# Attention and a squared-ReLU MLP in one kernel: transposes by row halves in the second half, other visits in the MLP

## The chip, the cores and the metric

The kernel runs on one core of a Trainium2 chip. The metric is the device time in microseconds (us) of one launch. TensorE is called PE here (its weight loads PEld), VectorE DVE, ScalarE ACT, GpSimd POOL, and SP is the engine that issues most DMAs. Each engine takes its instructions in the order of its own queue.

## The reference, cut to what matters

Four batches, eight heads, 576 positions, head size 64. A bias that depends on the distance of two positions goes through a tiny network (1 to 32 to 8) and is added to the scores; softmax; product with v. The result, 2304 tokens by 512, goes through a two-layer MLP with ReLU and a square between.

```python
scores = scale * np.matmul(q, k.transpose(0, 1, 3, 2)) + bias
attn = np.exp(scores - np.max(scores, axis=-1, keepdims=True))
x = np.matmul(attn / (attn.sum(-1, keepdims=True) + 1e-9), v)   # -> (2304, 512)
h = x @ w_in                                                   # (512, 2048)
out = np.maximum(h, 0) ** 2 @ w_out                            # (2048, 512)
```

## The kernel before, in words

**Attention.** An item is one batch, one pair of heads and one block of query rows. A full item has 128 rows of each of the two heads (two score tiles of 128x576); the last 64 rows of both heads make one tail item (one tile). Items are numbered by `s`. The first half (batches 0 and 1, items 0 to 39) also builds the bias. The second half (batches 2 and 3, items 40 to 79) takes its order from an explicit list: for each of eight groups (head pair, batch) four full items F and a tail T. Transposes and value products there go in pairs of items: at an even step `s`, after the scores of item `s`, PE transposes the exponentials of items `s-2` and `s-1`, ACT copies the results to SBUF (`pt`), and at step `s+1`, after the scores of item `s+1`, PE multiplies both with v (`px`). In ten items the pairs are FF, FF, TF, FF, FT, here named (0,1), (2,3), (T,0), (1,2), (3,T).

Four PSUM banks, tags a to d, serve the second half. Before, the four head groups of 128x128 transposes of a pair go to banks a, b, c and again a, the two blocks that straddle the heads (`pa`, L521) go to bank d, and `px` is written to bank d afterwards; DVE takes `px` out (L578). The scores hold four further banks, and only one item has room in them: the scores of the next item wait until DVE has read the last (L438). DVE writes its result to one of two buffers `t`, which ACT's exponential (L445) frees. In the first half, one item at a time, the transposes are already done by row halves (`transposes_by_rows`, `half_block`, L534): a 128x128 block is transposed as two blocks of 64 rows, from rows 0 to 63 into one bank and from rows 64 to 127 into another.

**Jobs.** Between these steps the second half runs a list of jobs, filled into each step by a budget of ACT and DVE time (`fill`): scanning w_in for its largest value, the normalisation of each group, the splitting of early w_in tiles (`in_job`: `lead`, `sums_in`, `high_in`, `low_in`) and of two w_out tiles (`out_job`) into a high and a low part, and the splitting of x of batches 0 and 1 (`x_scaled`: sums on POOL, high parts on ACT, low parts on DVE). A destination of such a part lies in the bias area and is free only when the items that read that bias are done (`dest_at`).

**MLP.** An item of the MLP, a visit, is one batch `n` of 256+256 tokens (or the tails of all) and one `P`: two w_in tiles of 128x512 and two w_out tiles. `products` does 42 matmuls of 256 columns (a seven-product scheme for 2x2 blocks, each operand in a high and a low part), `sums` (ACT and DVE) combines them, `squares` (ACT) does ReLU and square, `parts_g` splits the result (`gh` on ACT, `gl` on DVE), and `down` does 24 matmuls of 512 columns into `y`. In iteration `i` PE does `products(i)` and then `down(i-1)`. Beside them `lead_at` says which weight tile is prepared in an iteration, `largest_at` where the largest of an x is found, `split_at` where an x is split. A batch is visited twice where not all weights are there yet: `runs` lists batch, first P, end P. The w_in tiles that are not early are fetched one at a time into one buffer (`zw`), each after `low_in` of the one before.

Of the kernel before, what the change touches and what calls it, by code (L numbers as in the profile page):

```python
# [10 lines left out]
F32 = mybir.dt.float32  # L11
# [37 lines left out]
NE = 8  # L49
# [28 lines left out]
def attention_then_relu2_mlp(ctx: ExitStack, tc: tile.TileContext, q, k, v, cols, w_in, w_out, psi, xmat, dist, out):  # L78
# [422 lines left out]
    def transposes(us, tags=None):  # L501
        next_tag = iter(tags) if tags else None
        groups = []
        pa = None
        for m, u in enumerate(us):
            p_of = p_t.pop(u)
            pt = att.tile([128, 9, 128], F32, name="pt", tag="pt", bufs=2)
            pt_t[u] = pt
            for h in range(2 if units[u][2] < TAIL else 1):
                groups.append((p_of, pt, h))  # L510
            groups.append((p_of, pt, None, m))
        if len(us) > 1:
            heads = [g for g in groups if g[2] is not None]
            groups = heads[:3] + [g for g in groups if g[2] is None] + heads[3:]
        last = []
        for p, pt, h, *m in groups:
            if h is None:
                if pa is None:
                    pa = bank("pa", "d" if tags and len(us) > 1 else next(next_tag) if tags else None)
                at = slice(128 * m[0], 128 * m[0] + 128)  # L520
                PE.transpose(pa[:, at], p[:, S - 64:S + 64], ident)  # L521
                last.append((pt[:, 8], pa[:, at]))
                if len(last) == len(us):
                    yield from last
            else:
                pp = bank("pp", next(next_tag) if tags else None)
                for c in range(4):
                    k0 = h * (S + 64) + 128 * c
                    PE.transpose(pp[:, 128 * c:128 * c + 128], p[:, k0:k0 + 128], ident)  # L529
                yield pt[:, 4 * h:4 * h + 4], pp.rearrange("p (c m) -> p c m", c=4)  # L530

# [4 lines left out]
    def transposes_by_rows(u):  # L536
# [11 lines left out]
        yield pt[:, 8], pa  # L548

# [433 lines left out]
    def norm_job(u):  # L983
# [6 lines left out]
            ("ROW", 0.24, lambda: st.update(rows=norm_copy(norm_rows(st["parts"], "cb"[row_step[1] - 1]))), u + TL + 1, lambda: now[0] % 2 == 0 and row_left()),  # L990
# [32 lines left out]
    def scaled(ps_col):  # L1023
        wscale.extend(power_of(ps_col))
        for n in range(AB):
            job(now[0] + 1, ("DVE", 0.16, lambda n=n: power_job(now[0] + 1, overall(xcols[n]), lambda c: x_scaled(n, c)), lambda n=n: sum(x[0] == n for x in x_found) == HP))

    xcols = [column(HP) for _ in range(AB)]
# [3 lines left out]
    def x_job(at, n):  # L1032
        job(at, *(("DVE", 0.67, lambda c=c: x_found.append((n, x_largest(n, xcols[n], (c,))))) for c in range(HP)))

    def x_scaled(n, ps_col):
        scale_of(n, ps_col)
        if n == 0:
            place_x = raw_tile("w2")
            free = [place_x[:, 512 * k:512 * k + 512] for k in range(2)]
            for k, ms in enumerate(((3, 1, 7), (4, 6), (2, 5))):  # L1040
                stages = []
                for m in ms:
                    if RIGHT[m][1]:
                        sum_at[m] = free[k].rearrange("p (c t) -> p c t", c=2)
                        stages.append(("POOL", 1.3, lambda m=m: sums_x(0, (m,))))
                    stages.append(("ACT", 0.71, lambda m=m: high_x(0, (m,))))
                    stages.append(("DVE", 0.74, lambda m=m: low_x(0, (m,))))
                jobs.insert(len(norms), [max(now[0], first[groups[AB * HP + AB]] + 1), stages])
        else:
            free = [a.rearrange("p (c t) -> p c t", c=2) for a in (take(1, 4480, 512), take(0, 9856, 512))]  # L1050
            for k, ms in enumerate(((3, 1, 7), (4, 6), (2, 5))):
                stages = []
                for m in ms:
                    if RIGHT[m][1]:
                        sum_at[n, m] = free[k]
                        stages.append(("POOL", 1.3, lambda m=m: sums_x(n, (m,))))
                    stages.append(("ACT", 0.71, lambda m=m: high_x(n, (m,))))
                    stages.append(("DVE", 0.74, lambda m=m: low_x(n, (m,))))
# [53 lines left out]
    with tc.manual_schedule():  # L1112
# [5 lines left out]
        for s in range(NA, NU + TL + 3):  # L1118
# [17 lines left out]
            if s % 2 == 0:  # L1136
# [3 lines left out]
                for m, c in enumerate(transposes(us, iter("bacb" if s == NA else "abca")) if us else ()):  # L1140
                    ACT.copy(*c)  # L1141
# [283 lines left out]
```

## Time and profile before

| | us |
|---|---|
| median of 3 runs | 696.8 (696.4 to 697.21) |
| the profiled execution | 697.57 |
| its span in the trace | 695.8 |
| PE busy | 676.8 (97%) |
| DVE busy | 549.9 (79%) |
| ACT busy | 473.2 (68%) |
| POOL busy | 196.5 (28%) |

The span runs from the first instruction to the last; the execution's time holds 1.8 us more around it. Busy is the time in which an engine had at least one instruction under way. Matmuls overlap each other, so that PE is called busy also where the next matmul starts late; rates are therefore read from the starts of instructions.

### The profile page before, as it was taken

To read this page: it belongs to the slowest core of one execution; us is meant where nothing else is said; L and a number is where in the kernel's file an instruction comes from. 1 tells how busy PE (TensorE), PEld (TensorE's weight loads), DVE (VectorE), ACT (ScalarE), POOL (GpSimd) and SP (SyncE) were. 2 spreads that over 40 slices of the span, in tenths; PEclk is the share of its full clock that TensorE was granted. 3 is DMA by queue.
4 is the path that set the end of the run, shared out by engine and by line. 5 is a ranking of instruction groups with operands and counts; after the bars stand their busy time and mean duration, and the time that the engine had idled before them with its cause. 6 is when DMAs were issued, how large, how long until landed. Compare 5 with 4: busy or idle time off the path is not lost.

```text
span 695.8 us, 17950 instructions
## 1 busy us (share of the span) xinstructions
PE 676.8 (97%) x7238; PEld 561.5 (81%) x7238; DVE 549.9 (79%) x1165; ACT 473.2 (68%) x960; POOL 196.5 (28%) x313
## 2 busy tenths in 40 slices
PE   6899999999999999999999999999999999999997
PEld 5578888887877878778788888888888888888886
DVE  8999989877788898998888969777477775567664
ACT  5678888888777989997666756766466664447221
POOL 6465545442112343653223205112020112001000
PEclk9999999999999999999999999999999999999999
DMA  6740000017476134111901443050057222633101
GB/s 188 205 128 13 20 2 3 2 63 206 152 266 196 55 116 131 47 33 57 367 2 62 152 167 122 14 214 1 1 194 291 106 77 106 227 121 122 62 1 31
DMA packets 31682, 75.16 MB, mean 108 GB/s; under 512 B 5616, under 2 KB 13936, under 8 KB 30576
## 3 DMA queue, kind: packets, MB, share of 16 engines
q1 hardware_dynamic: 31440, 73.76, 31.1%
q8 instruction: 57, 0.93, 0.6%
q14 instruction: 25, 0.20, 0.1%
q10 hardware_dynamic: 160, 0.26, 0.1%
HBM read 55.66 MB, written 18.35 MB: 106 GB/s over the span
## 4 chain that ended last, share of the span: by engine, by line
PE 86%; DVE 8%; ACT 2%; issue 2%; POOL 1%; DMA 0%; ACTq 0%; POOLq 0%; DVEq 0%
PE y L1302 29%; PE ha L1210 13%; PE sp L425 11%; PE px L565 10%; PE hb L1210 10%; PE bb L383 5%; PE pp L529 3%; PE pp L534 3%; DVE t L438 2%; DVE mask L373 1%; PE pa L547 1%; ACT pt L1141 1%; DVE bt L391 1%; ACT p L445 1%; DVE xT L496 0%
## 5 line engine op out<-in xcount | busy, mean ns | idle before, releaser
L1210 PEld LDWEIGHTS <-area 128*128 128x128 f16 x1680 | 147.7, 98 | 25.3 <-issue 8.4
L1302 PE MATMUL y<-w,gh 128*128 128x512 f32 x576 | 149.0, 398 | 0.6 <-ACT gh L1246 0.6
L1302 PEld LDWEIGHTS y<-w,gh 128*128 128x128 f32 x576 | 105.1, 188 | 22.2 <-ACT gh L1246 1.3
L438 DVE CUSTOM_DVE_ANT_0 t<-sp,area 128x576 f32<-128x576 f32 x144 | 104.2, 753 | 21.2 <-PE sp L425 10.3
L445 ACT ACTIVATE p<-t,negm 128x576 f32<-128x576 f32 x144 | 112.9, 794 | 2.7 <-DVE negm L438 2.1
L425 PE MATMUL sp<-k,q 64*128 64x288 f32 (+1 forms) x640 | 99.4, 428 | 5.5 <-DVE negm L438 3.9
L565 PE MATMUL px<-pt,v 128*64 128x128 f32 (+1 forms) x1600 | 92.2, 266 | 0.0
L565 PEld LDWEIGHTS px<-pt,v 128*64 128x64 f32 x1600 | 79.2, 137 | 10.7 <-ACT pt L1141 6.0
L1210 PE MATMUL ha<-area 128*128 128x256 f16 (+1 forms) x816 | 85.1, 260 | 0.7 <-DVE c L1227 0.7
L399 POOL TENSOR_TENSOR area<-bt,bt 128x256 f32<-128x256 f32 x72 | 65.9, 922 | 64.1 <-DVE bt L391 63.9
L1302 PE MATMUL y<-w,gl 128*128 128x512 f32 x288 | 79.0, 390 | 0.0
L425 PEld LDWEIGHTS sp<-k,q 64*128 64x128 f32 (+1 forms) x640 | 53.3, 176 | 25.5 <-issue 6.0
L1210 PE MATMUL hb<-area 128*128 128x256 f16 (+1 forms) x612 | 64.7, 260 | 0.0
L1302 PEld LDWEIGHTS y<-w,gl 128*128 128x128 f32 x288 | 54.1, 188 | 12.2 <-DVE gl L1247 0.2
L373 DVE TENSOR_TENSOR mask<-sdist,theta 128x1024 f16<-128x1024 f16 x81 | 57.3, 711 | 1.0 <-PE bb L383 0.8
L869 ACT COPY pt<-pp 128x512 f32<-128x512 f32 (+1 forms) x76 | 37.4, 544 | 24.9 <-PE pp L534 24.7
L383 PEld LDWEIGHTS <-mask 128*128 128x128 f16 x1296 | 45.9, 99 | 9.5 <-DVE mask L373 6.4
L383 PE MATMUL bb<-wmov,mask 128*128 128x64 f16 x1296 | 47.5, 193 | 5.5 <-DVE mask L373 4.7
L1141 ACT COPY pt<-pp 128x512 f32<-128x512 f32 x76 | 41.4, 601 | 12.8 <-PE pp L529 12.3
L1247 DVE TENSOR_TENSOR gl<-area,gh 128x512 fp32r<-128x512 f32 (+1 forms) x40 | 25.3, 668 | 27.3 <-ACT gh L1246 25.5
L738 POOL TENSOR_TENSOR raw<-wa 128x256 f32<-128x256 f32 x16 | 12.2, 761 | 120.9 <-issue 66.1
L388 ACT ACTIVATE bt<-bb,small 128x256 f32<-128x256 f32 x81 | 39.1, 486 | 7.1 <-PE bb L383 5.2
(164 smaller groups left out, 1062.2 us busy)
## 6 DMA issues: line engine op xcount, KB each, us to landing
raw<-in_w_in SPq DMA_DIRECT2D x32, 512.0 KB, 4.4
r<-in_w_out SPq DMA_DIRECT2D x16, 512.0 KB, 5.4
xs<-area SPq DMA_DIRECT2D x4, 1792.0 KB, 11.1
py<-o SPq DMA_DIRECT2D x12, 512.0 KB, 4.1
o<-py SPq DMA_DIRECT2D x12, 512.0 KB, 4.1
v<-in_v SPq DMA_DIRECT2D x16, 320.0 KB, 4.0
q<-in_q SPq DMA_DIRECT2D x32, 128.0 KB, 3.0
out<-o SPq DMA_DIRECT2D x8, 512.0 KB, 2.9
```

The lines of the kernel that those rows point to most:

```text
L373: DVE.tensor_tensor(out=out, in0=win, in1=th, op=ALU.is_ge)
L383: PE.matmul(bb[:, 64 * (7 - r):64 * (8 - r)], lhsT=m[:, r], rhs=wmov[:, n], start=(n == 0), stop=(n == 1))
L388: ACT.activation(out=sv, in_=bv[:, 1], func=AF.Identity, scale=bscale)
L399: POOL.tensor_tensor(out=dst, in0=tw, in1=sw, op=ALU.add)
L425: mm = PE.matmul(out_t[to, x, :HALF], lhsT=qt[rows, cols], rhs=kt[rows, k0:k0 + HALF], start=True, stop=True)
L438: DVE.tensor_tensor_reduce(out=t.rearrange("p (x n) -> p x n", x=2), in0=sp[:, :, :HALF], in1=bias.rearrange("p (x n) -> p x n", x=2), sca ...
L445: ACT.activation(out=p[:, S * n:S * n + S], in_=t, func=AF.Exp, bias=negm[:, n:n + 1], scale=-1.0, accum_out=sums[:, 2 * ic + n:2 * ic + n ...
L565: PE.matmul(px[64 * h:64 * h + 64, 128 * m:128 * m + w], lhsT=vt[:, c, h], rhs=src, start=(c == 0), stop=(c == 4))
L869: ACT.copy(dst, src)
L1141: ACT.copy(*c)
L1210: PE.matmul(h[:, s, :w], lhsT=a, rhs=x, start=(k == 0), stop=(k == 5))
L1302: PE.matmul(y_t[n][k], lhsT=(gl if m == 2 else gh)[:, slot, o:o + 128], rhs=wl if m == 1 else wh, start=((n, P) in firsts and f == 0 and m ...
```

## The change

1. In the second half `transposes` goes, and `pair_by_rows` takes its place: 32 (FF) or 24 (FT) transposes of 64 rows, of item one into banks a and b, of item two into c and d; then the two `pa` blocks into bank a. ACT's copies keep their number; those of a tail are two of 256 elements instead of one of 512. The row products of the normalisation use banks c and d instead of c and b.
2. Six early tiles of w_in instead of eight; tiles 12 and 13 are prepared in the MLP, where 14 and 15 come later.
3. The largest of x of batch 1 and its splitting move from the jobs to the MLP's iterations 0 to 2; those of batches 2 and 3 move two and three iterations earlier, and each split starts in the iteration that works out its scale, one iteration sooner after it than before.
4. The visits: 3, 3, 3, 5, 2, 2, 5, 3, 3, 3 for batches 0, 1, 2, 3, 2, 1, 0, 1, 2, 3, before 4, 4, 4, 6, 2, 2, 4, 2, 2, 2; still 32, and 8 for the tails.
5. POOL's `high_in` multiplies by 1.0 as a second operation.

```diff
-NE = 8
+NE = 6
@@ in place of transposes
+    def pair_by_rows(us, tags):
+        pts = []
+        for m, u in enumerate(us):
+            p = p_t[u]
+            pt_t[u] = att.tile([128, 9, 128], F32, name="pt", tag="pt", bufs=2)
+            pts.append(pt_t[u])
+            pp = [bank("pp", tag) for tag in tags[2 * m:2 * m + 2]]
+            n = 8 if units[u][2] < TAIL else 4
+            for c in range(n):
+                for x in range(2):
+                    half_block(pp[x][:, 64 * c:64 * c + 64], p, x, c // 4 * (S + 64) + c % 4 * 128)
+            for x in range(2):
+                yield pts[m][:, :n, 64 * x:64 * x + 64], pp[x][:, :64 * n].rearrange("p (c m) -> p c m", c=n)
+        pa = bank("pa", tags[0])
+        for m, u in enumerate(us):
+            PE.transpose(pa[:, 128 * m:128 * m + 128], p_t.pop(u)[:, S - 64:S + 64], ident)
+        for m, pt in enumerate(pts):
+            yield pt[:, 8], pa[:, 128 * m:128 * m + 128]
@@ high_in
-                eng.tensor_scalar(out=hi, in0=src, scalar1=wscale[0], scalar2=None, op0=ALU.mult)
+                eng.tensor_scalar(out=hi, in0=src, scalar1=wscale[0], scalar2=1.0, op0=ALU.mult, op1=ALU.mult)
@@ norm_job
-            ("ROW", 0.24, lambda: st.update(rows=norm_copy(norm_rows(st["parts"], "cb"[row_step[1] - 1]))), ...
+            ("ROW", 0.24, lambda: st.update(rows=norm_copy(norm_rows(st["parts"], "cd"[row_step[1] - 1]))), ...
@@ x_scaled: the branch of batch 1 goes
-            for k, ms in enumerate(((3, 1, 7), (4, 6), (2, 5))):
...
-                job(dest_at[-1] + 1, *stages)
-    dest_at = [50] + [60] * 6 + [70]
-    order = list(early[:7]) + [2, early[7], 3]
+    dest_at = [50] + [60] * (NE - 1)
+    order = list(early[:NE - 1]) + [2, early[NE - 1], 3]
-        x_job(NA + 4, 0)
-        x_job(NA + 7, 1)
+        x_job(NA + 4)
-                for m, c in enumerate(transposes(us, iter("bacb" if s == NA else "abca")) if us else ()):
+                for c in pair_by_rows(us, "bacd" if s == NA else "abcd") if us else ():
@@ the MLP
-    runs = [(0, 0, 4), (1, 0, 4), (2, 0, 4), (3, 0, 6), (2, 4, 6), (1, 4, 6), (0, 4, 8), (1, 6, 8), (2, 6, 8), (3, 6, 8), (B, 0, 8)]
+    runs = [(0, 0, 3), (1, 0, 3), (2, 0, 3), (3, 0, 5), (2, 3, 5), (1, 3, 5), (0, 3, 8), (1, 5, 8), (2, 5, 8), (3, 5, 8), (B, 0, 8)]
-    lead_at = {1: (6, 7), 2: (10, 11), 3: (14,), 4: (15,)}
-    lead_at.update({5: (16,), 9: (17,), 12: (20,), 13: (21,), 14: (18, 19), 15: (22, 23)})
-    lead_at.update(zip(range(18, 26), ((n,) for n in range(24, 32))))
+    lead_at = {1: (6, 7), 2: (10, 11), 3: (12,), 5: (13,), 6: (16,), 8: (17,), 20: (22, 23), 21: (26, 27), 22: (30, 31)}
+    lead_at.update(zip(range(10, 20), ((n,) for n in (14, 15, 18, 19, 20, 21, 24, 25, 28, 29))))
-    ahead = {3: 15}
-    split_at.update({i + j: (n, ms) for i, n in ((6, 2), (10, 3), (30, B)) for j, ms in enumerate(((2, 5, 3, 4), (1, 6, 7)))})
-    largest_at = {4: 2, 8: 3, 28: B}
+    split_at.update({i + j: (n, ms) for i, n in ((1, 1), (4, 2), (7, 3), (30, B)) for j, ms in enumerate(((2, 5, 3, 4), (1, 6, 7)))})
+    largest_at = {0: 1, 3: 2, 6: 3, 28: B}
```

## Rows read from the trace of the kernel before

**Rows 1.** Windows: stretch, length, busy (count) of PE, PEld, DVE, ACT, POOL; clock, DMA

```profile
184.29:314.09 129.80, 126.59 (x1487) 101.59 (x1485) 116.68 (x296) 114.62 (x282) 49.73 (x104) 1.00 0.38 120
314.09:340.41 26.32, 25.03 (x251) 21.03 (x251) 22.05 (x43) 18.11 (x35) 9.68 (x14) 1.00 0.48 172
340.41:440.97 100.56, 100.56 (x661) 84.27 (x661) 83.48 (x127) 66.45 (x89) 24.65 (x21) 1.00 0.29 116
```

**Rows 2.** Timeline (start, us, engine, line), second half: PE over two pairs

```profile
266.81 1.53 PE L529 MATMUL pp<-ident,p 128*128 128x128 f32 x12
...
268.93 1.24 PE L425 MATMUL sp<-k,q 64*128 64x288 f32 x8
...
272.43 1.24 PE L425 MATMUL sp<-k,q 64*128 64x288 f32 x8
...
273.61 1.53 PE L529 MATMUL pp<-ident,p 128*128 128x128 f32 x12
...
274.97 0.38 PE L521 MATMUL pa<-ident,p 128*128 128x128 f32 x2
...
275.42 1.24 PE L425 MATMUL sp<-k,q 64*128 64x288 f32 x8
...
278.71 1.24 PE L425 MATMUL sp<-k,q 64*128 64x288 f32 x8 [0.22 <-DVE negm L438]
```

**Rows 3.** Timeline, the second of these pairs: ACT and DVE

```profile
274.35 1.56 ACT L1141 COPY pt<-pp 128x512 f32<-128x512 f32 x3 [0.86 <-PE pp L529]
...
276.10 0.82 ACT L445 ACTIVATE p<-t,negm 128x576 f32<-128x576 f32 x1
...
277.05 0.76 DVE L438 CUSTOM_DVE_ANT_0 t<-sp,area 128x576 f32<-128x576 f32 x1 [0.97 <-ACT p L445]
```

**Rows 4.** Timeline, first half: one item, transposed by row halves

```profile
123.40 1.24 PE L425 MATMUL sp<-k,q 64*128 64x288 f32 x8
...
124.47 0.66 PE L534 MATMUL pp<-ident,p 64*128 64x64 f32 x16
...
125.07 0.33 PE L547 MATMUL pa<-ident,p 128*128 128x128 f32 x1
...
125.23 1.07 ACT L869 COPY pt<-pp 128x512 f32<-128x512 f32 x2 [0.59 <-PE pp L534]
```

**Rows 5.** Groups by form (count, busy us, mean ns): a tail's copies, first half

```profile
L869 ACT COPY pt<-pp 128x256 f32<-128x256 f32 x16 | 5.2, 376 | 6.7 <-PE pp L534 6.6
```

**Rows 6.** Timeline, PE, from attention to MLP: its two marked waits

```profile
328.87 2.68 PE L1210 MATMUL ha<-area 128*128 128x256 f16 x23 [0.69 <-DVE c L1227]
...
334.70 2.13 PE L1302 MATMUL y<-w,gh 128*128 128x512 f32 x8 [0.60 <-ACT gh L1246]
```

**Rows 7.** Timeline, MLP iterations 4 to 6: DVE

```profile
369.02 2.46 DVE L204 TENSOR_REDUCE small<-xT 128x1 f32<-128x512 f32 x4
...
374.99 0.42 DVE L197 TENSOR_SCALAR wa<-wa 128x512 f32<-128x512 f32 x1
...
377.24 0.74 DVE L1226 SCALAR_TENSOR_TENSOR area<-ha,small,area 128x512 f32<-128x512 f32 x1
...
380.00 0.15 DVE L221 TENSOR_SCALAR small<-hb 128x1 f32<-128x1 f32 x1
...
380.81 1.58 DVE L756 SCALAR_TENSOR_TENSOR area<-wa,small,area 128x256 f16<-128x256 f32 x1
...
384.13 1.28 DVE L1247 TENSOR_TENSOR gl<-area,gh 128x512 fp32r<-128x512 f32 x2
...
388.09 2.73 DVE L810 SCALAR_TENSOR_TENSOR area<-xT,small,area 128x512 f16<-128x512 f32 x4
```

**Rows 8.** Timeline, the same iterations: POOL's sums and ACT's high parts of a split

```profile
379.56 2.55 POOL L797 TENSOR_TENSOR xT<-xT 128x512 f32<-128x512 f32 x2
...
385.04 2.55 ACT L803 ACTIVATE area<-xT,small 128x512 f16<-128x512 f32 x4
```

**Rows 9.** DMA issues: count, KB each, median us to landing

```profile
raw<-in_w_in SPq DMA_DIRECT2D x32, 512.0 KB, 4.4
```

More of the change, by code (lines that the diff above doesn't have):

```diff
@@ L499, in scale_x @@
         times_rows(b, hp, *spread_rows(rows_t))
[L501 to L530, printed above, removed]
     def half_block(dst, p, x, k0):
@@ L1024, in scaled @@
         wscale.extend(power_of(ps_col))
-        for n in range(AB):
-            job(now[0] + 1, ("DVE", 0.16, lambda n=n: power_job(now[0] + 1, overall(xcols[n]), lambda c: x_scaled(n, c)), lambda n=n: sum(x[0] == n for x in x_found) == HP))
-    xcols = [column(HP) for _ in range(AB)]
+        job(now[0] + 1, ("DVE", 0.16, lambda: power_job(now[0] + 1, overall(xcols), x_scaled), lambda: len(x_found) == HP))
+    xcols = column(HP)
     x_found = []
-    def x_job(at, n):
-        job(at, *(("DVE", 0.67, lambda c=c: x_found.append((n, x_largest(n, xcols[n], (c,))))) for c in range(HP)))
@@ L1035, in x_scaled @@
[L1035 to L1039, printed above, removed]
-            for k, ms in enumerate(((3, 1, 7), (4, 6), (2, 5))):
[L1041 to L1058, printed above, removed]
-                job(dest_at[-1] + 1, *stages)
@@ L1061, in attention_then_relu2_mlp, with x_job, x_scaled @@
-    dest_at = [50] + [60] * 6 + [70]
-    order = list(early[:7]) + [2, early[7], 3]
-    raw_of = dict(zip(early, ("stage", "stage", "zw", "w3", "stage", "stage", "zw", "stage")))
-    after = {early[0]: early[4], early[1]: early[5], early[2]: early[6], early[3]: 3, early[4]: early[7]}
+    def x_job(at):
+        job(at, *(("DVE", 0.67, lambda c=c: x_found.append(x_largest(0, xcols, (c,)))) for c in range(HP)))
+    def x_scaled(ps_col):
+        scale_of(0, ps_col)
+        place_x = raw_tile("w2")
+        free = [place_x[:, 512 * k:512 * k + 512] for k in range(2)]
+        for k, ms in enumerate(((3, 1, 7), (4, 6), (2, 5))):
+            stages = []
+            for m in ms:
+                if RIGHT[m][1]:
+                    sum_at[m] = free[k].rearrange("p (c t) -> p c t", c=2)
+                    stages.append(("POOL", 1.3, lambda m=m: sums_x(0, (m,))))
+                stages.append(("ACT", 0.71, lambda m=m: high_x(0, (m,))))
+                stages.append(("DVE", 0.74, lambda m=m: low_x(0, (m,))))
+            jobs.insert(len(norms), [max(now[0], first[groups[AB * HP + AB]] + 1), stages])
@@ L1065, in attention_then_relu2_mlp @@
+    dest_at = [50] + [60] * (NE - 1)
+    order = list(early[:NE - 1]) + [2, early[NE - 1], 3]
+    raw_of = dict(zip(early, ("stage", "stage", "zw", "w3", "stage", "stage")))
+    after = {early[0]: early[4], early[1]: early[5], early[3]: 3}
     fetched = {}
@@ L1331, in attention_then_relu2_mlp @@
             one, *two = lead_at.get(i, (None,))
-            if one is not None and one not in ahead.values():
+            if one is not None:
                 lead(one)
@@ L1356, in attention_then_relu2_mlp @@
                 low_x(*split_at[i])
-            if i in ahead:
-                lead(ahead[i])
             if i + 1 in split_at:
```

2 lines of the change are left out of this document (1 added, 1 removed).

## The prediction

> **What bounds the kernel now.** I read the windows first, to see in which stretch which engine has time to give. Through the second half of attention PE is busy for 126.59 of 129.80 us, DVE for 116.68 and ACT for 114.62; from the third MLP visit on PE is busy without a hole, 100.56 of 100.56, and DVE for 83% of it [rows 1]. So in the MLP every microsecond that PE waits ends up in the time, and none can be won there, since the change leaves its matmuls as they are. What can be won is in the 156 us before, and what can be lost is DVE time in the first MLP visits. PE's rate there is 661 matmuls in 100.56 us; a visit has 42 + 24 = 66, so a visit takes 10.04 us.
>
> Next comes the timeline of PE over two pairs of the second half [rows 2]. An FF pair runs from 266.81 to 273.61, 6.80 us, and PE has no marked wait in it: it is bound by PE's own work. The TF pair behind it has less for PE to do, but at 278.71 the scores wait for DVE. ACT and DVE of the same pair say why [rows 3]: ACT starts copying the transposes 0.74 after PE began them, needs 1.75 for the copies (274.35 to 276.10), then does the exponential; DVE's reduction of the next item idles 0.97 until that exponential gives back a buffer `t`; two reductions later the scores may start, 5.10 after the transposes did. With 1.18 from scores to transposes (272.43 to 273.61) that is a ring of 6.28 us which no faster transpose shortens, except by letting ACT start earlier. For an FF pair with full items behind it the same ring holds one more copy (1.56 for three, so 0.52): 6.80. PE's bound and the ring's thus lie close together, and I expect the ring to be late next.
>
> **Part 1, the transposes.** The first half shows the new form [rows 4]: 16 halves, one full item, go out in 0.60 us (124.47 to 125.07). Before, an FF pair takes 2.12 from its first transpose to the next scores (266.81 to 268.93) [rows 2]. After: 2 x 0.60 = 1.20, but `pa` now goes to bank a, which ACT must have copied out: ACT starts 0.76 after the first transpose (124.47 to 125.23), one copy of the two takes 0.54 [rows 4], so bank a is free at 1.30; from `pa` to the scores is 0.45 (274.97 to 275.42) [rows 2]. 1.75 in all, 0.37 less. Where no row product stands between, the scores before the transposes also end sooner, 1.07 (123.40 to 124.47) against 1.18; about half of the pairs, so 0.42 for an FF pair that PE binds.
>
> Of the 19 pairs that begin in the stretch, 12 are FF. In four of these, the pairs (0,1), two full items stand behind, and the ring of 6.80 (6.69 with the shorter scores) holds; I take 0.2. The other eight give 8 x 0.42 = 3.4, these four 0.8. In the seven FT and TF pairs the ring decides: where the tail comes first ACT starts 0.3 earlier (half of 0.60 for its transposes), but two copies of 0.376 [rows 5] replace one of 0.52, 0.23 more; where it comes second, only the 0.23 more is left. I take nothing for the seven. Sum: 4.2 us less. The ends: if only PE counted, and bank a cost nothing, FF would gain 2.12 - 1.65 + 0.11 = 0.58 and FT 1.81 (273.61 to 275.42) - 1.35 = 0.46, together 10.2; if ACT is mostly late, `pa` waits and holds the next scores behind it on PE, those hold DVE's reduction, and nothing is left of it: 0.
>
> The jobs that leave the second half (two tiles of w_in, the search and split of batch 1) free DVE of about 2 x (2.25 + 1.2) + 2.46 + 7 x 0.68 = 14 us (the prices are worked out in part 3), and ACT and POOL as well. The ring waits for ACT's copies and exponentials, not for these jobs, so I price this relief at nothing beyond what part 2 takes. POOL's second factor in `high_in` also costs nothing: POOL works 49.73 of 129.80 us [rows 1], and the tiles wait for their destination anyway; if that cover went, six operations would each come later by at most their own length, in a stage that is now free of the eighth tile. The new banks of the row products change no count. Bank d, which item two now needs at once, has to be emptied by DVE's copy of `px`; where DVE is late that takes part of the 0.42, and is why I don't go beyond 4.2.
>
> **Part 2, from attention to the MLP.** This stretch is 26.32 us with PE busy for 25.03 [rows 1]; the 1.29 between is two waits, 0.69 for DVE's sums of visit 0 and 0.60 for ACT behind them [rows 6]. With no tile and no split left over there, DVE and ACT reach those sums at once: I take both waits away, and 0.4 + 0.3 for the two pairs that fall in the stretch. 2.0 us less; the ends are 0.5 (the waits stay, since visit 1 follows visit 0 with no `down` between) and 2.8.
>
> **Part 3, DVE in visits 1 to 8.** The prices on DVE [rows 7]: preparing a weight tile 2.25 (374.99 to 377.24), the sums of a visit 2.76 (to 380.00), a scale 0.81 (to 380.81), the low parts of a w_in tile 3.32 (to 384.13), both `gl` 1.28, four low parts of x 2.73 and three 2.05, the largest of an x 2.46. The 3.32 was taken beside POOL's sums for a split (2.55 for two, begun at 379.56) [rows 8]; by elements, 896 against 512 in 0.68, it would be 1.2. I keep both. A plain visit costs 2.76 + 1.28 = 4.04.
>
> Visit 1: 4.04 + 2 x 2.25 + 0.81 + 2.73 = 12.1. Visit 2: 4.04 + 4.50 + 2.05 = 10.6. Visit 3: 4.04 + 2.25 + 1.2 to 3.3 + 2.46 = 10.0 to 12.1. Visit 4: 7.6. Visit 5: 9.5 to 11.6. Visits 6, 7 and 8 as 3, 4 and 5. Against 10.04 of PE, the first three run over by 2.7 to 4.8; visit 4 gives 2.4 back to DVE but not to PE, and visits 5 and 6 take up to 3.7. So PE waits between 2.7 (no collisions, no slack) and about 6. To this comes ACT: its four high parts, 2.55 [rows 8], now wait for the scale of the same visit and stand ahead of `squares`, so that `gh` and with it `down` come later in visits 1, 4 and 7; by up to 1 each beyond what DVE costs already. Against it: before, visits 1 to 3 carry 4.04 + 4.50 = 8.5 on DVE and PE shows no hole [rows 1], so some slack exists, perhaps 2. I take 5 us more; the ends are 1 and 8.5.
>
> Here a rule of the Trainium skill bears on the size. The row is that a low part of 256 elements took 1.58 while POOL's sums ran [rows 7, 8]. The page "SBUF — State Buffer", section "SBUF: two separate sides", says that DVE operations with two SBUF inputs and GpSimd share one pair of ports by an exclusive lock, held for the whole instruction. The row agrees with it as far as one collision goes. By that rule every POOL sum of the splits can cost DVE its full length, 13 x 1.28; this is the second rival below, priced there from rows.
>
> **Part 4, later visits.** Visits 14 to 19 prepare six w_in tiles in a row from one buffer; fetch 4.4 [rows 9], preparation 2.25, sums 2.76 and low parts 1.2 make 10.6, over 10.04. A lag of 0.6 for each of five would be 3 us; the queues ahead of PE should take most of it. 0.5, between 0 and 3.
>
> **The sum.** -4.2 - 2.0 + 5.0 + 0.5 = -0.7, against the profiled execution's 697.57 (695.8 of span, 1.8 around it). That execution is 0.8 above the median of 696.8, so I forecast 696.1.
>
> **Rivals.**
> 1. The MLP hides its bill: PE's queue and the empty hand-over give DVE a start, part 3 costs 1. Then -4.2 - 2.0 + 1.0 = -5.2: 691.6. For it: 8.5 per visit went without a wait before. Against: 12.1 in visit 1, when `gl` of visit 0 can't be early.
> 2. Slower: DVE binds the first eight visits, because POOL's 13 sums of splits (1.28 each, 16 us in all) collide with its low parts and `gl`. Part 3 costs 8.5, part 4 1.0: -4.2 - 2.0 + 9.5 = +3.3, so 700.1. It decides from a bill of about 7 on in part 3, where the whole turns to +1.4. For it: 3.32 instead of 1.2 in [rows 7]. Against: POOL was busy for only a quarter of that stretch.
> 3. The row halves don't do what they say: `pa` in bank a stands behind a late ACT, part 1 gives 1: +2.5, so 699.3. Against: in the first half ACT was idle when the halves came (0.59) [rows 4].
> 4. PE binds every pair, part 1 gives 9: -5.5, so 691.3. Against: the wait of 0.97 [rows 3].
>
> **How the numbers follow.** The forecast has 0.42 (its own range 694 to 698.3), the rivals in order 0.20, 0.26, 0.06 and 0.06. A measurement tells no change up to about 0.2%, 1.4 us. Of the forecast's 0.42, 0.12 is faster, 0.28 same, 0.02 slower; rivals 1 and 4 give 0.25 faster and 0.01 same; rival 2 0.24 slower and 0.02 same; rival 3 0.05 slower and 0.01 same. Faster 0.37, same 0.32, slower 0.31. The range goes from 691.0 to 700.8.
>
> **What would show it.** Part 1: FF pairs of about 6.4 between their first transposes, TF pairs still near 6.3, `pa` waiting for ACT's first copy. Part 2: no wait of PE for L1227 at visit 1. Part 3: holes of PE in visits 1 to 3, at L1210's `hb` for DVE's low parts and at L1302 for `gh`, of 2 us and more. Part 4: ACT's preparation waiting for the fetch from visit 15 on. I am wrong if PE shows no hole after visit 2, or if pairs of both kinds fall below 6.2.

## The result and the profile after

The changed kernel takes 704.02 us (median of 4 runs, 703.59 to 704.48) against 696.76 for the kernel before: ratio 1.0099 [1.0087, 1.0111], 7 us slower. The profiled execution has a span of 701.6; that of before has 695.8. These spans differ by 5.8 and not by 7, since the profiled execution of before is 0.8 above its median.

The windows of after; columns as in [rows 1]. The first two are cut at the same places as there, the third ends where the products of visit 9 start, and the fourth follows it.

```profile
183.77:312.01 128.24, 119.37 (x1760) 92.26 (x1758) 110.05 (x282) 111.87 (x284) 41.52 (x99) 1.00 0.34 114
312.01:337.03 25.02, 24.80 (x281) 20.22 (x280) 15.53 (x33) 14.38 (x29) 2.69 (x9) 1.00 0.46 159
337.03:417.68 80.65, 74.11 (x467) 60.83 (x466) 73.05 (x120) 55.87 (x81) 31.57 (x28) 0.98 0.34 131
417.68:696.00 278.32, 278.30 (x1973) 234.29 (x1973) 189.04 (x327) 145.71 (x206) 29.30 (x38) 1.00 0.30 106
```

The second half of attention takes 128.24 instead of 129.80: 1.6 won, although PE is busy 7.2 us less. The way to the products of visit 2 takes 25.02 instead of 26.32: 1.3 won. The seven visits from there to the products of visit 9 take 80.65. Before, the same stretch took 71.05: 9.6 lost.

```profile
340.41:411.46 71.05, 71.05 (x466) 59.36 (x465) 58.73 (x91) 45.83 (x62) 15.62 (x13) 1.00 0.30 119
```

Behind it 283.9 instead of 284.3, and the first half, which the change leaves alone, ends 0.5 earlier. Sum: -0.5 - 1.6 - 1.3 + 9.6 - 0.4 = +5.8, the difference of the spans.

The starts of the products give the time of each visit. Visits 5, 6 and 8 take 10.07, 10.08 and 10.06; visit 2 takes 14.32, visit 3 12.71, visit 4 11.29, visit 7 12.12: over 10.08 by 4.2, 2.6, 1.2 and 2.0. PE's marked waits in them (start, us, engine, line, what; in brackets the idle time and what ended it):

```profile
343.81 3.68 PE L1274 MATMUL y<-w,gh 128*128 128x512 f32 x8 [2.03 <-ACT gh L1218]
...
355.69 1.48 PE L1182 MATMUL hb<-area 128*128 128x256 f16 x12 [1.44 <-DVE area L798]
358.04 0.70 PE L1182 MATMUL hb<-area 128*128 128x256 f16 x5 [0.87 <-DVE area L798]
...
369.42 0.38 PE L1300 MATMUL hb<-small,ones 128*128 128x1 f32 x2 [0.59 <-DVE small L204]
...
401.68 0.38 PE L1300 MATMUL hb<-small,ones 128*128 128x1 f32 x2 [1.42 <-DVE small L204]
```

In visit 2 the `gh` of visit 1 is late, and the eight matmuls behind that hole take 3.68, at a granted clock of 0.52 (more on this in the last section); in visit 3 the low parts of batch 1; in visits 4 and 7 the matmul that spreads the largest of batch 2 and 3 over the partitions, which stands between `products` and `down`, waits for DVE's search. The other three engines around the first wait:

```profile
338.14 2.56 ACT L791 ACTIVATE area<-xT,small 128x512 f16<-128x512 f32 x4 [1.96 <-DVE small L224]
...
342.67 3.41 POOL L785 TENSOR_TENSOR xT<-xT 128x512 f32<-128x512 f32 x2 [4.47 <-DVE area L798]
...
343.79 2.84 DVE L1219 TENSOR_TENSOR gl<-area,gh 128x512 fp32r<-128x512 f32 x2 [0.53 <-ACT gh L1218]
```

ACT waits 1.96 for the scale and then makes four high parts, with `squares` and `gh` queued behind. POOL's two sums and DVE's `gl` then run into each other: 3.41 instead of 2.55 [rows 8], 2.84 instead of 1.28 [rows 7]. Such a meeting need not cost time: the kernel before has one as long (DVE, then POOL), and PE has no marked wait there.

```profile
391.05 3.13 DVE L1247 TENSOR_TENSOR gl<-xT,gh 128x512 fp32r<-128x512 f32 x2 [0.23 <-ACT gh L1246]
390.24 3.40 POOL L797 TENSOR_TENSOR xT<-xT 128x512 f32<-128x512 f32 x2 [6.72 <-DVE area L810]
```

Two pairs of attention, PE, to be laid beside [rows 2]:

```profile
266.31 1.22 PE L503 MATMUL pp<-ident,p 64*128 64x64 f32 x32
267.75 0.44 PE L534 MATMUL pa<-ident,p 128*128 128x128 f32 x2 [0.22 <-ACT pt L1115]
268.11 1.24 PE L425 MATMUL sp<-k,q 64*128 64x288 f32 x8
...
272.69 0.93 PE L503 MATMUL pp<-ident,p 64*128 64x64 f32 x24
...
274.52 1.24 PE L425 MATMUL sp<-k,q 64*128 64x288 f32 x8 [0.39 <-DVE negm L438]
...
279.19 1.02 PE L503 MATMUL pp<-ident,p 64*128 64x64 f32 x21
```

The FF pair takes 6.38 (was 6.80), the TF pair 6.50 (was 6.34), and PE now waits once for ACT (0.22) and once for DVE (0.39).

### The profile page after: what moved, and what is told of

It is laid out like the page before. It is cut to its first block, busy times and chain, and to the rows that moved or that the text cites. A ratio compares the mean times of both kernels' runs of the same rounds, so it can differ in the third digit from the quotient of the medians.

```text
span 701.6 us, 18564 instructions
## 1 busy us (share of the span) xinstructions
PE 673.1 (96%) x7542; PEld 554.4 (79%) x7542; DVE 547.9 (78%) x1165; ACT 473.1 (67%) x970; POOL 191.6 (27%) x311
## 4 chain that ended last, share of the span: by engine, by line
PE 45%; DVE 5%; DMA 1%; issue 0%; ACT 0%
PE y L1274 25%; PE ha L1182 11%; PE hb L1182 8%; DVE area L744 1%; DVE small L204 1%; DMA raw<-in_w_in 1%; DVE area L798 0%; DVE wa L200 0%; DVE wa L201 0%; DVE gl L1219 0%; DVE wa L198 0%; DVE area L1201 0%; DVE area L1200 0%; DVE wa L197 0%; DVE area L1198 0%
## 5 line engine op out<-in xcount | busy, mean ns | idle before, releaser
L1182 PE MATMUL ha<-area 128*128 128x256 f16 (+1 forms) x768 | 79.7, 260 | 0.2 <-DVE c L1199 0.2
L1182 PE MATMUL hb<-area 128*128 128x256 f16 (+1 forms) x576 | 60.8, 259 | 2.3 <-DVE area L798 2.3
L503 PEld LDWEIGHTS pp<-ident,p 64*128 64x128 f32 x1144 | 45.0, 140 | 11.8 <-issue 1.9
L383 PEld LDWEIGHTS <-mask 128*128 128x128 f16 x1296 | 48.1, 102 | 7.7 <-DVE mask L373 5.5
L857 ACT COPY pt<-pp 128x512 f32<-128x512 f32 (+1 forms) x76 | 37.4, 544 | 24.8 <-PE pp L503 24.5
L383 PE MATMUL bb<-wmov,mask 128*128 128x64 f16 x1296 | 49.6, 197 | 4.0 <-DVE mask L373 3.7
L503 PE MATMUL pp<-ident,p 64*128 64x64 f32 x1144 | 49.2, 226 | 0.7 <-DVE xT L566 0.4
L1115 ACT COPY pt<-pp 128x512 f32<-128x512 f32 (+1 forms) x83 | 39.5, 557 | 15.2 <-PE pp L503 14.9
```

Source lines behind the costliest of these rows:

```text
L383: PE.matmul(bb[:, 64 * (7 - r):64 * (8 - r)], lhsT=m[:, r], rhs=wmov[:, n], start=(n == 0), stop=(n == 1))
L503: PE.transpose(dst, p[rows, k0:k0 + 128], ident[rows, rows])
L857: ACT.copy(dst, src)
L1182: PE.matmul(h[:, s, :w], lhsT=a, rhs=x, start=(k == 0), stop=(k == 5))
```

## Experiments: the MLP

Each time is a ratio to the kernel before, run beside it, with its 95% interval. "Visits 2 to 9" is the stretch between the products of these visits, 71.05 before and 80.65 after.

**x1_jobs.** The changed kernel, batch 1 back among attention's jobs:

```diff
-    for i, n in ((1, 1), (4, 2), (7, 3), (30, B))
+    for i, n in ((4, 2), (7, 3), (30, B))
-    largest_at = {0: 1, 3: 2, 6: 3, 28: B}
+    largest_at = {3: 2, 6: 3, 28: B}
+        x_job(NA + 7, 1)    # and x_scaled(1, ...) as before, its stages from step 71
```

> The changed kernel with the largest and the whole splitting of batch 1 back among attention's jobs (sums, high and low parts from step 71 on, as in the kernel before); six early tiles, the new visits, the splits of batches 2 and 3 and the row halves stay. Theory A (batch 1's search and split, moved into visits 0 to 2, make the waits of visits 2 to 4: 4.2 + 2.6 us): these waits go, 6 to 7 us come back, up to 1.5 of it is lost again at the end of attention: 697 to 699. Holes of 0.6 and 1.4 at the scale's matmul in visits 4 and 7 stay. Rival E (the w_in and w_out tiles of visits 1 to 3 overload DVE by themselves, whatever batch 1 does): PE still waits in visits 2 and 3, and no more than 3 us come back: 701 or more.

1.0018 [1.0008, 1.0028], 698.59. Visits 2 to 9: 74.27, so 6.4 came back; visits 2 and 3 take 10.08 and 10.09. Theory A. What is left are the scale's matmuls in visits 4 and 7, one behind the visits that search:

```profile
363.32 0.38 PE L1314 MATMUL hb<-small,ones 128*128 128x1 f32 x2 [0.71 <-DVE small L204]
395.95 0.38 PE L1314 MATMUL hb<-small,ones 128*128 128x1 f32 x2 [1.77 <-DVE small L204]
```

**early_scales** adds to it a search one visit earlier, and prepares the tiles 13, 16 and 17 one to two visits later:

```diff
-    largest_at = {3: 2, 6: 3, 28: B}
+    largest_at = {2: 2, 5: 3, 28: B}
-    lead_at = {..., 3: (12,), 5: (13,), 6: (16,), 8: (17,), ...}
+    lead_at = {..., 3: (12,), 6: (13,), 8: (16,), 9: (17,), ...}
```

> The changed kernel with batch 1's search and split among attention's jobs, the largest of batches 2 and 3 found one visit earlier (visits 2 and 5 in place of 3 and 6, so that the scale is known a visit ahead of the split, as in the kernel before) and tiles 13, 16, 17 prepared one to two visits later (6, 8, 9 in place of 5, 6, 8); visits, six early tiles and row halves stay. Theory A (all of the MLP's loss is batch 1 in visits 0 to 2, 6.4, and a scale asked for in the visit that splits, 3.6): no wait of PE in visits 2 to 9, which take 70.6 to 71, and 694 to 695.5, faster than before by 2 to 3 and as fast as the row halves alone or up to 1 faster. Rival E3 (splits and tiles closer together overload DVE in any order): PE waits 2 us or more in visits 3 to 8, 696.5 to 698.

0.9985 [0.9976, 0.9994], 695.78: now faster than before. Visits 2 to 9: 72.10. Of the 3.2 that x1_jobs still lost, 2.2 came back; visits 3 and 4 keep 0.6 and 0.7 (a wait of 0.28 for `gh`). Theory A, with a rest: the time lies just above its range. Search and tiles moved together, so their shares of the 2.2 are not shown.

**largest_first** leaves the visits of the changed kernel alone and only moves the search ahead of the tile's low parts.

```diff
+            if i in largest_at:
+                scales.append(overall(x_largest(largest_at[i])))
             if one is not None:
                 (sums_in if is_in(one) else high_out)(one)
...
-            if i in largest_at:      # was behind low_in, low_x and sums_x
-                scales.append(overall(x_largest(largest_at[i])))
```

> The changed kernel with one edit: in the visits that look for the largest of an x, DVE does that search directly behind the visit's sums, ahead of the low parts of the weight tile, so that PE's matmul for the scale finds it done in the next visit. No work is added or taken away. Theory A (the waits of 0.59 and 1.42 in visits 4 and 7 are an order in queues: a matmul with a late operand stands between products and down): both waits go, visits 4 to 5 and 7 to 8 are at 10.1 again, 3 us come back: 700.5 to 702. Rival F (DVE is overloaded by sheer work there, and what is brought forward pushes something else behind): the hole moves to hb or gh of the same or the next visit, 703.5 to 704.5.

1.0088 [1.0074, 1.0102]. Both waits went; visit 4 took 10.52 (0.8 less), visit 7 only 0.5 less, because `gh` was late instead, behind the four high parts that still wait for the scale, and visit 6 took 0.3 more:

```profile
401.17 2.14 PE L1274 MATMUL y<-w,gh 128*128 128x512 f32 x8 [1.07 <-ACT gh L1218]
```

Mostly rival F. Searching a few us earlier is no cure; early_scales, where the scale is known a visit before the split, got more back.

**scale1_jobs** asks what batch 1's 6.4 are: only its search and scale go back to attention (`largest_at` without visit 0, the split still in visits 1 and 2).

> The changed kernel with only the search for the largest of batch 1 and its scale back among attention's jobs; the split itself (sums on POOL, high parts on ACT, low parts on DVE) stays in visits 1 and 2. It tells the order from the work in the 6.4 us that batch 1 costs. Theory A1 (order: ACT's high parts wait for the scale of the same visit and stand ahead of squares, so gh is late): the wait of 2.03 at visit 2 falls to under 0.5, 2 to 3 us come back, the waits for low parts at visit 3 shrink too: 699.5 to 702. Rival E2 (work: DVE's low parts and gl beside POOL's sums are too much for the visit whenever the scale comes): waits of 4 us or more stay in visits 2 and 3, 702 to 704.

1.01 [1.0085, 1.0116]: nothing gained, and above the ranges of both. The wait for `gh` went, but the low part of w_out tile 7 (`rest_out`), queued on POOL behind the sums of the next split, came 2.92 late, and behind that hole PE ran at half its clock. PE's wait, then the windows from it on (last columns: clock, DMA):

```profile
347.66 3.35 PE L1278 MATMUL y<-w,gh 128*128 128x512 f32 x7 [2.92 <-POOL w L713]
```
```profile
345.00:347.60 2.60, 0.00 (x0) 0.00 (x0) 2.56 (x2) 0.00 (x0) 2.60 (x2) 0.83 0.00 0
347.60:350.00 2.40, 2.34 (x6) 1.86 (x7) 2.40 (x4) 1.76 (x4) 1.07 (x2) 0.50 0.02 7
350.00:352.50 2.50, 2.50 (x7) 1.61 (x5) 2.36 (x6) 2.47 (x5) 0.22 (x1) 0.50 0.00 0
```

**scale1_out_first** moves `sums_x(*split_at[i + 1])` behind `high_out` of the second tile.

> The kernel of scale1_jobs with one change of order: POOL's sums for the next visit's split are queued behind the low part of the second w_out tile (rest_out) and no longer ahead of it. No work is added or taken away. In scale1_jobs PE waits 2.92 for that low part (347.66), and the granted clock is 0.50 for some 5 us behind the wait. Theory A1 (order): the wait goes and the clock stays at 1.00 there, visit 2 falls from 15.5 to 10.1 to 11, 4 to 5.5 us come back: 698.5 to 700.5; the wait of 1.7 in visit 7 stays. Rival E2 (DVE and POOL are short of time there in any order): PE waits as long for c, hb or gh in visits 2 and 3, 703 or more.

1.0089 [1.0076, 1.0102]. The clock stayed up and POOL's low part came in time, yet visit 2 took 13.47. DVE's `gl` of visit 1, now beside POOL's sums for its whole length, took 3.47 instead of 1.28; tile 10 and the visit's own sums came behind it, and PE waited for these sums. Rival E2, except for the clock. DVE, then PE:

```profile
342.51 3.47 DVE L1223 TENSOR_TENSOR gl<-area,gh 128x512 fp32r<-128x512 f32 x2
...
350.72 2.79 PE L1186 MATMUL ha<-area 128*128 128x256 f16 x24 [2.41 <-DVE c L1203]
```

**no_x1_sums** takes POOL's sums for batch 1 away.

```diff
+            op = op if n != 1 else None
             yield cs, op, half[one[1]]...
```

> The changed kernel in which POOL's five sums for the split of batch 1 are left out (the high and low parts of batch 1 are made of one operand instead of a sum or difference, so that part of the computation is changed); ACT's and DVE's instructions keep their number, shape and order. Rival 2 of the prediction (POOL's sums collide with DVE's low parts and gl and make them twice as long): gl of visit 1 takes 1.3 instead of 2.84, the second low parts 2.0 instead of 2 x 2.43, and 3 to 5 us of batch 1's 6.4 come back: 699 to 701. Theory W (DVE's own work is too much for visits 1 to 3, with or without collisions): 702 to 704; the wait of 2.03 for gh at visit 2 stays by either, since ACT still waits for the scale.

1.0067 [1.0054, 1.0081], 2.2 us less than the changed kernel. Visit 2 took 12.37 (was 14.32); the others are unchanged. `gl` took 1.96 with only `rest_out` beside it:

```profile
344.51 1.96 DVE L1220 TENSOR_TENSOR gl<-area,gh 128x512 fp32r<-128x512 f32 x2 [0.53 <-ACT gh L1219]
344.53 2.12 PE L1275 MATMUL y<-w,gh 128*128 128x512 f32 x8 [2.03 <-ACT gh L1219]
```

Between the two theories: with the late scale still there, the five sums for batch 1 are worth 2.0, a fifth of the MLP's loss. The sums for batches 2 and 3 are still made.

**scale1_no_sums** takes the late scale and the sums away together.

> The kernel of scale1_jobs (the largest and the scale of batch 1 worked out in attention, its split in visits 1 and 2) in which POOL's five sums for batch 1 are left out, so that part of the computation is changed. Late scale and collisions are both gone, ACT's and DVE's work for the split stays. Theory C (late scale and collisions make up the 6.4): visits 2 to 4 take 30.3 to 31.8 against 38.3 in the changed kernel, waits for hb under 0.5, 697.5 to 699.5 (the waits in visits 4 and 7 for batches 2 and 3 stay). Theory W (DVE's work in visits 1 to 3 is too much by itself): 33 or more for visits 2 to 4, 700.5 or more, with PE waiting at hb for low parts.

1.0025 [1.0015, 1.0035], 698.8. Visit 2 takes 10.17: late scale and sums are all of its 4.2. Each hides part of the other: taking only the sums away gave 2.0, and with the early scale of scale1_out_first (13.47) they are worth 3.3. Visit 3 takes 12.71, as in the changed kernel, with the same waits (PE, then DVE and POOL):

```profile
350.91 1.48 PE L1187 MATMUL hb<-area 128*128 128x256 f16 x12 [1.45 <-DVE area L799]
353.25 0.71 PE L1187 MATMUL hb<-area 128*128 128x256 f16 x5 [0.87 <-DVE area L799]
...
350.11 3.09 DVE L799 SCALAR_TENSOR_TENSOR area<-xT,small,area 128x512 f16<-128x512 f32 x3
...
350.92 1.73 POOL L713 TENSOR_TENSOR w<-wa,w 128x512 fp32r<-128x512 f32 x1 [3.68 <-DVE area L799]
```

From 334 us on DVE has no marked idle time in this trace until these low parts (350.11 to 353.1): two tiles, sums, `gl` and low parts in each of two visits. So theory C for visit 2. In visit 3 theory W explains the first wait, 1.45. The second, 0.87, follows another collision that this edit leaves in: the three low parts take 3.09 beside POOL's `rest_out`, where four took 2.73 [rows 7], so 2.05 for three.

**ordered** keeps batch 1's split in the MLP, in visits 0 and 1 instead of 1 and 2, with the scale from attention, the order of scale1_out_first and the visits of early_scales.

> As scale1_out_first, and besides: batch 1 is split in visits 0 and 1 instead of 1 and 2, the largest of batches 2 and 3 is found in visits 2 and 5, and tiles 13, 16, 17 are prepared in visits 6, 8, 9. All of batch 1's split stays in the MLP, as in the changed kernel; only its place and the order differ. Theory A1 (the 10 us are order, not work): visits 2 to 9 take 70.6 to 73, 694 to 697. Rival E2 (work): 698.5 or more, with PE waiting for DVE's low parts or sums in visits 1 to 4.

1.002 [1.0011, 1.0029]. Visits 2 to 9: 74.43, so 6.2 came back with batch 1's split still in the MLP; PE waits 1.50 for the search of batch 2 in visit 3. Between the ranges: with the same work in the MLP but for the search of batch 1, another place and order give back nearly two thirds of the 9.6.

## Experiments: attention

**rows_alone.** The kernel before with `pair_by_rows` and row products in banks c and d.

> The kernel before with part 1 alone: pair_by_rows in place of transposes, and the row products in banks c and d; visits, early tiles and the splits as before. Theory A (the gain of part 1 is real but small, because ACT's copies, its exponential and DVE's reduction keep the pairs apart; the loss of the whole change lies in the MLP): 693.5 to 695.5, faster than before by 1.5 to 3, the stretch from item 40 to the last pair shorter by about that, and no wait of PE in the MLP's first nine visits. Rival B (part 1 does nothing by itself, and the 1.6 us that the changed kernel gains in attention come from the jobs that left it): 696.5 to 697.2. Rival C (PE binds the pairs, and something else in the changed kernel ate the gain): under 691.

0.998 [0.9971, 0.9989], 1.4 us faster. Theory A, at 695.62 just above its range. The pairs are within 0.2 of the changed kernel's but for three (7.00 for 7.62, 7.32 for 6.91, 7.11 for 6.25), where other jobs lie beside them.

**mlp_alone.** The changed kernel with the old transposes.

> The changed kernel with part 1 undone: the old transposes, four banks and pa in bank d, the row products in c and b; the new visits, six early tiles and the split of batch 1 in the MLP stay. Theory A: the MLP's loss of 10 us stays whole, visits 2 to 9 take about 80.6, and attention loses what the row halves gave: 705.5 to 707. Rival B (the attention gain came from the jobs that left): 704 to 704.5, as the changed kernel. Rival D (the row halves let the MLP begin differently, and the holes of the first visits depend on that): the stretch from visit 2 to visit 9 changes by more than 1 us against the changed kernel's 80.65.

1.0117 [1.0103, 1.0131], 705.6. Visits 2 to 9: 80.67. Theory A: the two parts add, and the holes don't depend on attention.

**rows_pa_dve** and **early_scales_pa_dve.** DVE takes `pa` out of PSUM, behind its two reductions.

```diff
-                    ACT.copy(*c)
+                    pas.append(c) if len(c[1].shape) == 2 else ACT.copy(*c)
             for fn in sms:
                 fn()
+            for o, i in pas:
+                DVE.tensor_copy(out=o, in_=i)
```

> The kernel before with the row halves, and DVE instead of ACT takes the straddling blocks pa out of PSUM (two copies of 128 elements per pair), behind its two reductions of the item. It shortens ACT's part of the ring copies, exponential, reduction, scores by 0.46 per pair and adds as much to DVE. Theory A (ACT stands last in most pairs): up to 0.4 for each of the 19 pairs, 3 to 6 us less than the row halves alone: 689.5 to 692.5. Rival G (PE and DVE are as late as ACT, the ring has no single bound): 694.5 to 696, as the row halves alone. Rival H (DVE binds): 696.5 or more.

> Both edits together: the changed kernel with batch 1 among attention's jobs, early scales and later tiles, and DVE takes the straddling blocks out of PSUM. Theory A: the two gains add, 688.5 to 692. Rival G: 694 to 695.5. Rival H: 696 or more.

1.0089 [1.0075, 1.0103] and 1.0035 [1.0022, 1.0047]: 7.6 and 3.7 us more than without the edit: the times of rival H. DVE's waits for the exponential are nearly gone (0.4 instead of 6.8), but its copies now wait for PE's `pa` with all of DVE's work behind them. Waits of DVE (us in all, times, longest), first of rows_alone, then of rows_pa_dve:

```profile
DVE t L438 <- ACT p L445: 6.8, 8, 1.7
```
```profile
DVE pt L1139 <- PE pa L534: 6.3, 12, 0.9
...
DVE t L438 <- ACT p L445: 0.4, 1, 0.4
```

**rows_px_act.** The reverse: ACT copies `px` (0.42 per pair), `ACT.copy(dst, src)` for `keep_values`.

> The kernel before with the row halves, and ACT instead of DVE takes the value products px out of PSUM (a copy of 0.42 per pair, at the end of the odd step). It is the reverse of rows_pa_dve, where 0.49 per pair went from ACT to DVE and the whole took 7.6 us longer than the row halves alone. Theory H (DVE stands last in most pairs): 3 to 6 us less than the row halves alone, 689.5 to 692.5. Rival G (a ring through PE, ACT and DVE without a single bound: what is moved from one to the other is paid there): 694.5 to 697. Rival K (ACT binds, and in rows_pa_dve only the place in DVE's queue cost): 698 or more.

0.9979 [0.9971, 0.9988], as rows_alone. Rival G, and against H: what DVE saves, ACT and then PE's wait for bank d pay. DVE waits 8.8 for the exponential instead of 6.8, and PE for ACT's copy out of bank d:

```profile
PE pp L503 <- ACT xT L1144: 2.9, 5, 0.8
```

**pa_late.** PE does `pa` behind the scores of the next item; `reduce` of the item is issued ahead of these scores, ACT's copies of `pa` still ahead of its exponentials.

> The kernel before with the row halves, and PE does the blocks pa behind the scores of the next item instead of ahead of them; ACT copies them where it did, ahead of the exponentials. PE then has nothing to wait for in bank a and starts those scores 0.4 to 1.0 earlier. Theory P (bank a's wait and pa's 0.44 on PE hold the pairs): 3 to 6 us less than the row halves alone, 689.5 to 692.5. Theory T (the ring through ACT's copies, its exponential, the buffers t and DVE's reduction holds, and scores that come sooner only wait for it): 694.5 to 697, with more waiting of DVE for the exponential.

1.018 [1.0166, 1.0194], 14 us more than rows_alone. The early scores won nothing; ACT, made to wait for `pa`, held back the exponential, and DVE waited for that. Waits of DVE, then of ACT:

```profile
DVE t L438 <- ACT p L445: 23.1, 17, 2.5
```
```profile
ACT pt L1137 <- PE pa L535: 14.3, 14, 2.2
```

Theory T's chain, though the loss is far above what it expected (709.65): DVE waits 16 us more for the exponential than in rows_alone.

**mixed_visits** joins the row halves, six early tiles and batch 1 in attention with visits of 3, 4, 4, 6, 2, 2, 5, 2, 2, 2 and a search two visits ahead of each split; **mixed_t3** adds a third buffer `t`.

```diff
-        t = att.tile([128, S], F32, name="t", tag="t", bufs=TB)
+        t_no[0] += u > 60
+        t = take(0, 8960, S) if u > 60 and t_no[0] % 3 == 0 else att.tile([128, S], F32, name="t", tag="t", bufs=TB)
```

> The changed kernel with batch 1's search and split among attention's jobs, visits of 3, 4, 4, 6, 2, 2, 5, 2, 2, 2 and one weight tile in each of visits 3 to 6 (12, 13, 14, 15), the largest of batches 2 and 3 in visits 3 and 7, their splits from visits 5 and 9 on: row halves and six early tiles stay, and the visits are nearly those of before. Theory A (row halves give 1.5 to 2, six early tiles give 1.3 at the end of attention, and both stay if no visit is overfull): visits 2 to 9 take 70.6 to 71.2, 693.5 to 695, faster than before and than either part alone. Rival E3 (the freed jobs only move their cost into the visits): 695.5 to 697.

> The kernel of mixed_visits with a third buffer t between DVE's reduction and ACT's exponential for items 61 to 79, in a piece of the bias area that is free by then. Theory T (the two buffers t hold the pairs: DVE waits for the exponential to give one back): DVE's waits for it vanish in the last nine pairs, each gets 0.2 to 0.5 shorter, 2 to 4 us less than mixed_visits: 692 to 694.5. Theory P (PE with bank a holds them) or Rival G (several links as late as each other): within 0.8 of mixed_visits, 695.5 to 697.

0.9992 [0.9983, 1.0001] and 0.9978 [0.9968, 0.9989]. Visits 2 to 9 take 71.74 and 71.60, no marked wait in them. mixed_visits lies in the range of rival E3 all the same. The third buffer ended DVE's waits for the exponential (3.5 in four before), but DVE then waited for the scores (4.6 instead of 2.5), and attention got only 0.6 shorter. At 695.03, about 1 us below mixed_visits, mixed_t3 lies between the ranges of T and G, nearer to G; it has the lowest median here, but its interval overlaps those of rows_alone and rows_px_act. Waits of DVE from 245 us on, mixed_visits, then mixed_t3:

```profile
DVE t L438 <- ACT p L445: 3.5, 4, 1.5
...
DVE t L438 <- PE sp L425: 2.5, 4, 1.4
```
```profile
DVE t L441 <- PE sp L425: 4.6, 7, 1.5
```

mixed_visits also tells what made the search late in visits 4 and 7. Ahead of the search stand the low parts of a w_in tile. In the changed kernel they run beside POOL's sums for the next split; in mixed_visits, which splits a visit later, they run alone. DVE in visit 3 of the changed kernel, then of mixed_visits:

```profile
364.13 0.85 DVE L744 SCALAR_TENSOR_TENSOR area<-wa,small,area 128x256 f16<-128x256 f32 x1
364.90 1.90 DVE L744 SCALAR_TENSOR_TENSOR area<-raw,small,area 128x640 f16<-128x640 f32 x1
```
```profile
357.93 0.48 DVE L744 SCALAR_TENSOR_TENSOR area<-wa,small,area 128x256 f16<-128x256 f32 x1
358.33 0.88 DVE L744 SCALAR_TENSOR_TENSOR area<-raw,small,area 128x640 f16<-128x640 f32 x1
```

That is 1.4 us longer, more than the wait of 0.59 in visit 4. In mixed_visits the scale's matmul does not wait there, although the search stands behind the low parts as before; in x1_jobs, which also has batch 1 in attention, the low parts are as long as in the changed kernel (0.84 and 1.90) and the matmul waits 0.71. The low parts ahead of visit 7 are as long too (0.92 and 1.89), and PE waits 1.42. So the rows make these two waits collisions as well, though no run takes the sums for batches 2 and 3 away by themselves.

**mixed_last** adds the edit of largest_first to mixed_t3.

> The kernel of mixed_t3 in which DVE looks for the largest of an x directly behind a visit's sums, ahead of the low parts of the weight tile (the edit of largest_first). In mixed_t3 visit 3 takes 10.64, visit 6 10.25 and visit 8 10.41 instead of 10.08. If the late search of visit 3 is what PE waits for there, 0.3 to 0.6 come back: 694.2 to 695; if ACT's gh is (0.91 of DVE's idle time stands behind it), nothing: 694.8 to 695.4.

1.0023 [1.0013, 1.0033], a miss by both: about 3 us more than mixed_t3. The low parts of tile 12 came 2.6 later, the next tile is fetched into the same buffer only behind them, and ACT waited for it ahead of the visit's sums (visit 4, called visit 3 in the expectation: 12.95). ACT, then PE:

```profile
366.08 0.67 ACT L195 ACTIVATE wa<-raw 128x512 f32<-128x512 f32 x1 [3.13 <-DMA raw<-in_w_in]
...
370.50 1.70 PE L1200 MATMUL ha<-area 128*128 128x256 f16 x14 [2.16 <-DVE xT L1217]
```

## Why the prediction was wrong

It forecast -0.7 in all and a range up to 700.8; the sum came out at +5.8.

**Part 3 failed, and it decides.** "I take 5 us more; the ends are 1 and 8.5": the trace shows 9.6. The places were right: holes in visits 2 and 3, at `hb` for DVE's low parts and at `gh` for ACT behind the scale, of 2 us and more. Three things in the sizing were wrong.
- The account set DVE's time per visit against PE's 10.04 and let the good visits make up for the bad ("visit 4 gives 2.4 back"). It left out one instruction, PE's own matmul for the scale. That waits for the end of DVE's search with `down` queued behind it, in visits 4 and 7, which the account had at 7.6 each, under PE's time. These two visits lost 3.2; with the search a visit earlier and three tiles later, 2.2 of it came back (early_scales).
- "By up to 1 each beyond what DVE costs already" for ACT's high parts behind the scale. In visit 2 the scale held ACT for 1.96, and PE 2.03.
- The collisions were priced in the second rival, and the forecast held only the longer low parts of [rows 7], as the upper end for visits 3, 5, 6 and 8. But what a collision costs depends on what waits behind it. Batch 1's five sums are worth 2.0 in the changed kernel and 3.3 with an early scale. By the rows, `rest_out` adds up to 0.9 in visit 3, and the longer low parts make the search late in visits 4 and 7, where PE waits 2.0 in all. Only the 2.0 is shown by an edit in the changed kernel; the rest, an estimate from these waits, would bring collisions to about half of the 9.6. The rows of visit 2 agree with the rule weighed in the prediction (the Trainium skill, page "SBUF — State Buffer", section "SBUF: two separate sides") that one engine waits while the other holds the ports: `gl` took 2.84 and POOL's two sums 3.41, each longer than alone. By that rule the five sums could have cost 6.4 (5 x 1.28); 2.0 to 3.3 were measured.

The rival "slower" named the right sign and the right stretch with a bill of 8.5. Its mechanism, POOL's sums, is shown for a fifth of the loss and is likely behind more. Its chance was 0.26; the slack of "perhaps 2" that spoke for 5 covered none of these waits.

**Part 1: right in direction, mis-sized.** -4.2 forecast, -1.6 measured; alone it is worth 1.4 (rows_alone). The four pairs (0,1) gave 0.75 for 0.8. The eight others of kind FF were to give 3.4: seven gave 2.3, and the eighth, the first pair of the stretch, lost 1.1, since PE waits 0.78 there for POOL's part of a second row product. The seven FT and TF pairs, taken at nothing, lost 0.5. "FF pairs of about 6.4, TF pairs still near 6.3" was right (6.38 and 6.50), and so was `pa` waiting for ACT's first copy: 3.3 us in 12 waits. Of the 7.2 us that PE is busy less, 5.6 went into waits. Late ACT is shown to be one link (pa_late). The runs speak against a single link that holds the pairs: each of the four edits that relieved one (rows_pa_dve, rows_px_act, pa_late, mixed_t3) left most of the wait with another. Which shorter ring would pay is open.

**Part 2: right.** -2.0 forecast, -1.3 measured, and PE waits no more for the sums at visit 1; inside its ends.

**Part 4: the wait came, its cost did not.** +0.5 forecast, -0.4 measured, a little outside its ends; 0.3 of it because visit 9 no longer holds a scale's matmul. ACT's preparation waits for the fetch in visits 16 to 19, 1.30 to 2.20 each, as the prediction said, and PE has no marked wait behind them. The longest of the four:

```profile
513.46 0.67 ACT L195 ACTIVATE wa<-raw 128x512 f32<-128x512 f32 x1 [2.20 <-DMA raw<-in_w_in]
```

That one buffer can cost 2 to 3 us at once showed only in mixed_last.

The range failed since it added up DVE's time and left out what stands in the other queues behind a late operand: 9.6 is above the end of 8.5, and part 1, which should have paid for it, gave little over a third.

## What to carry to other kernels

Where an engine has a few us to spare per step, adding its time up is not enough: list, in each queue, every instruction whose operand comes from the added work, PE's one-column matmul included, and what stands behind it. The same list tells which collisions between two engines will be paid. A value that all later work of a step needs (a scale) is worked out one step before the step that uses it. When one engine of a ring is relieved by 5%, expect the next link to hold: moving work along the ring won nothing here, and moving it off the ring was not tried.

## What the runs showed of the hardware

The clock falls after holes that a tuned kernel makes by itself, and not every time. In the changed kernel PE stood still from 341.80 to 343.80; from 343.80 to 347.32 the granted clock was 0.52 (the level of 1.2 GHz for nearly all of it), and eight matmuls took 3.68. In largest_first and mlp_alone the same hole of 2.03 left the clock at 1.00; the same eight took 2.12. The time of that visit was the same (14.32, 14.34, 14.32): at full clock PE waited later in the visit instead, in largest_first 0.79 for POOL's low part and 0.73 for DVE's sums. In scale1_jobs the holes of 2.92 and 1.73 were both followed by a clock near 0.5, and visit 2 took 15.52, visit 7 13.97 against 12.45 in x1_jobs, which has a hole of 1.77 there and no fall.
